# Attention in key steps of 128 with the last 64 keys of two groups in quarters of the array, and a new order of mixing units and norm steps

## The chip, the core and the metric

One core of a Trainium2 chip runs the whole program. TensorE (PE) multiplies: weights are loaded (PEld) and a second operand streams past them into PSUM, which has eight banks. ScalarE (ACT), VectorE (DVE) and GpSimd (POOL) work on what is in SBUF, ACT and DVE on PSUM too; SyncE's queue (SP) issues the transfers. Each engine works through its own instructions in order and waits at semaphores for the others. The metric is the device time of one execution in microseconds (us); lower is better.

## What is computed

```python
scores = q @ k^T / sqrt(64) - log(448)         # 8 batches x 12 heads, 448 x 448, head size 64
attn   = sigmoid(scores)                       # no sum over keys: each key chunk stands alone
x      = attn @ v                              # put together as (8, 448, 768)
u      = x + real(fft over tokens(fft over channels(x)))
un     = (u - mean) / sqrt(var + 1e-6)         # over the 768 channels
out    = u + relu(un @ w_ch1) @ w_ch2          # 768 -> 3072 -> 768
```

## The kernel before

Two heads share the 128 partitions (head j on rows 64j to 64j+63); such a pair is a *group* g, 48 in all, and two groups make a *round* gg of four heads, three rounds to a batch. Queries are stored as 450 columns, since the transform wants tokens n and -n side by side.

**Scores.** `scores` (L124) takes one step t of 112 keys of one group. The operands are split into a high and a low part (`cast` L111 on ACT, `rest` L119 on DVE), and three products are summed: six matmuls at L131, the two heads in the two row halves of the array. Outputs lie in a two-bank PSUM tile `sc`, of which there are two; ACT's sigmoid (L135) turns it into `a`, of which there are six buffers.

**Values.** `values` (L138) follows every fourth step: four chunks of 112 keys times two heads at L148, plain fp32, 64 columns per head, so the two heads stand in the two column halves. Each such fp32 matmul is two instructions in the trace. ACT copies the sum to `xT` (L155).

**Mixing.** When a batch is through, `fold` (L159, POOL and DVE) forms sums and differences `xp`, and `mix_units` (L176) returns a list of small units: 24 `stage_d` (L181, one fp32 matmul each, with an ACT copy `A` after every six), 4 `stage_s` (L194, needing `A`; an ACT copy `Q` or two DVE operations), 8 `add_x` (L209, transposes and a DVE addition `u`, stored to `u_dram`). They share three PSUM tiles `m`. `mix_some` (L428) gives out units worth a budget in estimated us and carries what is not used over to the next call, up to one budget while the list is empty.

**Side work.** `weight` (L248) converts 48 pieces of the feed-forward weights during attention (a load, an ACT step, DVE steps at L268 to L277, a store). `norm` (L345) normalises the first 512 tokens; its step 7 scales rows on DVE and at once asks ACT for a half-precision copy `hl` (L363). `load_qk` (L98) has two buffers and is called three steps ahead of its cast.

**Order.** The loop at L503 writes out all queues: two score steps, then what is due by the table `extra` at these steps (`at`, L469), then in turn mixing units (2.5 us) or a group's values. `pin` (L440) fixes the order on each engine as written. After attention the units of the last batch are given out between the first feed-forward matmuls (L617); the rest of the program (three quarters of the time) is the feed-forward part, which the diff does not touch except for one buffer: the ring `ws` of pool `ws1` (L395), which holds prepared weights `wp`.

Of the kernel before, what the change touches and what calls it, by code (L numbers as in the profile page):

```python
# [18 lines left out]
S = 448  # L19
# [3 lines left out]
D = 64  # L23
DM = 768
DF = 3072
CP = 112
NG = 3
NFC = DF // 128
NCC = DM // 128
LAG = 2  # L30
ABUF = 6
FOLDS = ((10, 11, 13, 14, 18, 19), (18, 19, 20, 21, 22, 23), (24, 24, 25, 25, 26, 26))
LEAD = 4
LNT = 2
UNIT_US = 2.5
ADD_US = 0.5
HELD = 3

# [16 lines left out]
def spectral_attention_ffn(tc, q, k, v, w1, w2, cd, cs, ident_in, out):  # L55
# [8 lines left out]
    with ExitStack() as top:  # L64
# [19 lines left out]
        if True:  # L84
            c1 = mix.enter_context(tc.tile_pool(name="c1", bufs=1, side="right"))
            fx = mix.enter_context(tc.tile_pool(name="fx", bufs=1, side="right"))
            ps_m = mix.enter_context(tc.tile_pool(name="ps_m", bufs=3, space=PSUM, side="right"))
            io = att_ctx.enter_context(tc.tile_pool(name="io", bufs=2))
            wk = att_ctx.enter_context(tc.tile_pool(name="wk", bufs=2))
            ps_sc = att_ctx.enter_context(tc.tile_pool(name="ps_sc", bufs=2, space=PSUM))  # L90
            ps_av = att_ctx.enter_context(tc.tile_pool(name="ps_av", bufs=1, space=PSUM))

            cd_sb = c1.tile([128, 2, 2, 3, 193], F32, name="cd_sb")
            cs_sb = c1.tile([HM, 2, 2, HM], F32, name="cs_sb")
# [2 lines left out]

            def load_qk(g):  # L98
                b, n = divmod(g, 2 * NG)
                qr = io.tile([128, SQ], F32, tag="qr", name="qr")  # L100
                kr = io.tile([128, S], F32, tag="kr", name="kr")
                nc.sync.dma_start(kr, k[b, n])
                nc.sync.dma_start(qr, q[b, n])
                raw[g] = (qr, kr)

            def load_v(gg):
                b, r = divmod(gg, NG)
                vrs[gg] = vr = io.tile([CP, 4, 256], F32, tag="vr", name="vr")
                nc.sync.dma_start(vr, v[b, r])

            def cast(g, n, e=None):  # L111
# [12 lines left out]
            def scores(t):  # L124

                g, c = divmod(t, 4)
                ps = ps_sc.tile([128, 2, 512], F32, tag="sc", name="sc")
                for n, (kn, qn) in enumerate(((0, 0), (0, 1), (1, 0))):
                    for j in range(2):
                        h = slice(j * D, (j + 1) * D)  # L130
                        nc.tensor.matmul(  # L131
                            ps[:CP, j, :SQ], split[g, 1, kn][h, c * CP:(c + 1) * CP], split[g, 0, qn][h],
                            start=(n == 0), stop=(n == 2))
                att[g, c] = a = wk.tile([CP, 2, SQ], F32, tag="a", name="a", bufs=ABUF)
                nc.scalar.activation(  # L135
                    a, ps[:CP, :, :SQ], AF.Sigmoid, bias=-math.log(S), scale=1.0 / math.sqrt(D))

            def values(g):  # L138
                gg, pr = divmod(g, 2)
                b, r = divmod(gg, NG)  # L140
                p = r + 3 * pr
                vr = vrs[gg]
                ps = ps_av.tile([128, 512], F32, tag="av", name="av")
                for c in range(4):
                    a = att.pop((g, c))
                    for j in range(2):
                        h = 2 * pr + j
                        nc.tensor.matmul(  # L148
                            ps[j * D:(j + 1) * D, :SQ], vr[:, c, h * D:(h + 1) * D], a[:, j],
                            start=(c == 0), stop=(c == 3))  # L150
                if r == 0 and pr == 0:
                    xts[b] = (fx.tile([128, 6, 2, HS], F32, tag="xT", name="xT", bufs=2),
                              fx.tile([128, 2, 2, 2, 3, HM], F32, tag="xp", name="xp"))
# [22 lines left out]
            def mix_units(b):  # L176
# [32 lines left out]
                def add_x(kp, r, hf):  # L209
# [14 lines left out]
                    def add():  # L224
# [10 lines left out]
                    dve_next.append(add)  # L235


                res = [(0.33, lambda kp=kp, c=c, par=par, p=p: stage_d(kp, c, par, p))
                       for kp in range(2) for c in (1, 0) for par in range(2) for p in range(3)]
                res += [(0.65, lambda kp=kp, c=c: stage_s(kp, c)) for kp in range(2) for c in (1, 0)]  # L240
                res += [(ADD_US, lambda kp=kp, r=r, hf=hf: add_x(kp, r, hf))
                        for kp in range(2) for r in range(2) for hf in range(2)]
                return res

            wtile = {}
# [99 lines left out]
            def norm(c, i, n, pool):  # L345
                if n == 0:
                    u = pool.tile([128, DM, 2], F32, tag="un", name="un")
                    u = u.rearrange("p n w -> p (n w)").rearrange("p (i n) -> p i n", i=2)
                    r0 = c * TW + i * 128
                    nc.sync.dma_start(u, u_dram[r0:r0 + 256, :].rearrange("(i p) n -> p i n", p=128))  # L350
                    uns[c, i], uns[c, i + 1] = u[:, 0], u[:, 1]
                elif n == 1:
                    stats(c, i % 2, uns[c, i])
                elif n < 7:
                    rsqrt(c, n)
                elif n == 7:
                    u = uns[c, i]
                    scale_rows(c, i % 2, u)
# [4 lines left out]
                    nc.scalar.activation(hl[:, 0], u, AF.Copy)  # L363
                    uns[c, i] = u, hl
                else:
                    u, hl = uns.pop((c, i))
                    nc.vector.tensor_tensor(out=hl[:, 1], in0=u, in1=hl[:, 0], op=ALU.subtract)
                    for n in range(2):
                        nc.sync.dma_start(uts[c][n][:, :, i * 128:(i + 1) * 128], hl[:, n], transpose=True)

            def norm_plan(c, g, pool):

                res = [(0, lambda: norm(c, 2 * g, 0, pool))]
                for j in range(2):
                    i = 2 * g + j
                    res += [(LEAD + j, lambda i=i: norm(c, i, 1, pool)),
                            (7 + LEAD + 2 * j, lambda i=i: norm(c, i, 7, pool)),
                            (8 + LEAD + 2 * j, lambda i=i: norm(c, i, 8, pool))]
                res += [(LEAD + n, lambda n=n: norm(c, 2 * g, n, pool)) for n in range(2, 7)]
                return sorted(res, key=lambda x: x[0])  # L380

# [79 lines left out]
            if G > 2:  # L461
                load_qk(2)
            if GG > 1:
                load_v(1)
            TQ = 4 * G
            TP = TQ - 16
            extra = {}
# [4 lines left out]
            for b in range(B):  # L472
                for r, when in enumerate(FOLDS):
                    for n, t in enumerate(when):
                        e = nc.vector if r == 2 and n % 2 else nc.gpsimd
                        at(24 * b + LAG + t, lambda b=b, r=r, n=n, e=e: fold(b, r, n, e))
                at(24 * b + 27 + LAG, lambda b=b: units.extend(mix_units(b)))
            for gg in range(2, GG):
                at(8 * gg - 8 + LAG, lambda n=gg: load_v(n))
            for g in range(2, G):  # L480
                if g > 2:
# [427 lines left out]
def _layout(q, k, v, w1, w2):  # L909
# [4 lines left out]

    n = np.arange(HS)
    qt, kt = (np.ascontiguousarray(a) for a in (qt[..., np.concatenate([n, -n % S])], kt))
    vt = np.ascontiguousarray(v.reshape(B, 2, NG, 2, 4, CP, D).transpose(0, 2, 5, 4, 1, 3, 6)).reshape(B, NG, CP, 4, 256)
# [52 lines left out]
```

## Time and profile before

| | |
|---|---|
| median of 3 runs | 1672.88 us (1671.16 to 1675.73) |
| the profiled execution | 1672.65 us, span 1670.9 us, mean granted TensorE clock 0.991 |
| the last group of attention's values starts | 442.56 us |
| one ordinary batch in the middle of attention | 53.93 us |
| batches in which tokens are normalised | 61.61 and 61.62 us |

The time is a span plus a little around it. The page gives busy shares of the whole program; what an edit is worth has to be read in the stage it touches, which here is the first 446 us. In the views, "idle before <-releaser" says how long an engine stood still ahead of a group and what ended that.

### The profile page before, as it was taken

The page shows a single profiled execution, that of the slowest core. Times are in us where ns is not written, and L with a number is a line of the kernel's source. Part 1 is how long each engine was busy: PE and PEld are TensorE (multiplying, and loading weights), DVE is VectorE, ACT ScalarE, POOL GpSimd, SP SyncE. Part 2 cuts the span into 40 slices and gives each one's busy share as a digit, 9 for nine tenths or more (in the row PEclk, how much of TensorE's full clock was granted, in tenths as well). Part 3 has the DMA queues.
Part 4 walks back from the last instruction along what each step waited for, and adds up shares of the span by engine and source line. Part 5 has one row for each costly group of instructions (what it writes and reads, how often), then busy time and mean ns, then how long its engine had stood idle before and what let it go on. Part 6 is the DMA issues. An engine that isn't in the chain of part 4 may idle for free.

```text
span 1670.9 us, 28280 instructions
## 1 busy us (share of the span) xinstructions
PE 1612.0 (96%) x11272; PEld 1098.5 (66%) x11272; DVE 1317.4 (79%) x2548; ACT 696.8 (42%) x927; POOL 271.3 (16%) x224
## 2 busy tenths in 40 slices
PE   7999988899989999999999999999999999999998
PEld 3555555455545545777777777777777777777775
DVE  3887798877458875688888888888888888887778
ACT  5766766676544542432233223322332233223221
POOL 1323322322676762000000000000000000000000
PEclk9999999999999999999999999999999999999999
DMA  7777778676287687755665566556655665666561
GB/s 229 278 252 241 245 266 275 201 273 227 89 279 274 245 323 268 300 203 220 242 244 197 225 242 246 197 225 241 244 199 223 241 246 193 229 241 228 208 240 68
DMA packets 85174, 388.69 MB, mean 233 GB/s; under 512 B 14913, under 2 KB 28466, under 8 KB 66482
## 3 DMA queue, kind: packets, MB, share of 16 engines
q1 hardware_dynamic: 85042, 386.89, 63.8%
q8 instruction: 88, 1.44, 0.3%
q14 instruction: 44, 0.36, 0.1%
HBM read 311.36 MB, written 73.92 MB: 231 GB/s over the span
## 4 chain that ended last, share of the span: by engine, by line
PE 77%; DVE 11%; ACT 4%; DMA 3%; issue 3%; POOL 3%; SPq 0%; ACTq 0%; DVEq 0%; POOLq 0%
PE pso L781 28%; PE psf L725 28%; PE av L148 7%; PE sc L131 6%; PE psd L186 3%; POOL wq L409 3%; DVE wp L401 2%; PE po L555 2%; ACT a L135 2%; DMA qr<-q_in 1%; DVE u L225 1%; PE psh L535 1%; PE pst L654 1%; PE pss L197 1%; DVE wt L275 1%
## 5 line engine op out<-in xcount | busy, mean ns | idle before, releaser
L781 PE MATMUL pso<-ws,H 128*128 128x384 f16 x3024 | 507.5, 326 | 1.0 <-DVE H L731 0.9
L725 PE MATMUL psf<-ut,ws 128*128 128x256 f16 x4536 | 506.6, 273 | 1.1 <-DVE ur L576 1.1
L725 PEld LDWEIGHTS <-ws 128*128 128x128 f16 x4536 | 443.9, 98 | 60.2 <-issue 1.4
L781 PEld LDWEIGHTS <-H 128*128 128x128 f16 x3024 | 295.6, 98 | 186.9 <-DVE H L731 1.7
L750 ACT ACTIVATE F<-F 128x1024 f32<-128x1024 f32 x72 | 76.1, 1057 | 400.3 <-DVE F L731 400.3
L796 DVE TENSOR_TENSOR acc<-pso,acc 128x384 f32<-128x384 f32 x399 | 207.1, 549 | 21.6 <-PE pso L781 21.6
L731 DVE TENSOR_TENSOR H<-F,H 128x1024 f16<-128x1024 f32 (+1 forms) x144 | 155.3, 1087 | 54.0 <-ACT H L760 54.0
L135 ACT ACTIVATE a<-sc 112x900 f32<-112x900 f32 x192 | 166.5, 919 | 56.0 <-PE sc L131 56.0
L760 ACT ACTIVATE H<-F 128x1792 f16<-128x1792 f32 x72 | 122.2, 1697 | 106.6 <-DVE F L731 106.6
L731 DVE TENSOR_TENSOR F<-X,psf 128x256 f32<-128x256 f32 x288 | 117.4, 417 | 56.1 <-PE psf L725 52.6
L148 PE MATMUL av<-a,vr 112*64 112x450 f32 x768 | 157.0, 552 | 0.0
L409 POOL TENSOR_TENSOR wq<-wq 128x384 f32<-128x384 f32 x96 | 133.5, 1395 | 59.4 <-DVE wp L401 37.0
L731 DVE TENSOR_TENSOR F<-F 128x256 f32<-128x256 f32 x288 | 109.4, 421 | 20.2 <-ACT F L750 15.6
L399 ACT ACTIVATE wp<-wq,wsc 128x1536 f16<-128x1536 f32 x48 | 74.5, 1571 | 91.9 <-POOL wq L409 90.6
L148 PEld LDWEIGHTS av<-a,vr 112*64 112x64 f32 x768 | 51.2, 137 | 83.9 <-issue 82.5
L731 DVE TENSOR_TENSOR X<-X,psf 128x256 f32<-128x256 f32 x216 | 89.6, 415 | 17.3 <-PE psf L725 13.8
L401 DVE SCALAR_TENSOR_TENSOR wp<-wq,wsc,wp 128x1536 f16<-128x1536 f32 x48 | 92.8, 1959 | 11.9 <-ACT wp L399 11.8
L535 PE MATMUL psh<-ut,wp 128*128 128x512 f16 x432 | 100.1, 381 | 0.3 <-ACT U L655 0.3
L131 PE MATMUL sc<-qh,kh 64*112 64x450 f32 x384 | 82.6, 426 | 15.0 <-ACT a L135 10.6
L555 PE MATMUL po<-wp,hh 128*128 128x256 f16 (+1 forms) x384 | 90.0, 330 | 0.0
L739 ACT ACTIVATE X<-psf 128x256 f32<-128x256 f32 x72 | 27.8, 386 | 147.4 <-PE psf L725 147.4
L131 PEld LDWEIGHTS sc<-qh,kh 64*112 64x112 f32 x384 | 34.4, 176 | 71.2 <-issue 29.9
(84 smaller groups left out, 1679.5 us busy)
## 6 DMA issues: line engine op xcount, KB each, us to landing
ws<-w_dram SPq DMA_DIRECT2D x144, 1344.0 KB, 6.7
wr<-w_in SPq DMA_DIRECT2D x48, 768.0 KB, 6.2
w_dram<-wp SPq DMA_DIRECT2D x24, 1344.0 KB, 10.6
t_dram<-wt SPq DMA_DIRECT2D x48, 384.0 KB, 4.5
wq<-t_dram SPq DMA_DIRECT2D x24, 768.0 KB, 5.9
qr<-q_in SPq DMA_DIRECT2D x48, 225.0 KB, 4.9
kr<-k_in SPq DMA_DIRECT2D x48, 224.0 KB, 5.0
vr<-v_in SPq DMA_DIRECT2D x24, 448.0 KB, 4.1
```

The lines of the kernel that those rows point to most:

```text
L131: nc.tensor.matmul(ps[:CP, j, :SQ], split[g, 1, kn][h, c * CP:(c + 1) * CP], split[g, 0, qn][h], start=(n == 0), stop=(n == 2))
L135: nc.scalar.activation(a, ps[:CP, :, :SQ], AF.Sigmoid, bias=-math.log(S), scale=1.0 / math.sqrt(D))
L148: nc.tensor.matmul(ps[j * D:(j + 1) * D, :SQ], vr[:, c, h * D:(h + 1) * D], a[:, j], start=(c == 0), stop=(c == 3))
L401: nc.vector.scalar_tensor_tensor(out=w[:, 1, part], in0=t, scalar=sc, in1=w[:, 0, part], op0=ALU.mult, op1=ALU.subtract)
L409: nc.gpsimd.tensor_tensor(out=t[:, o], in0=t[:, x], in1=t[:, y], op=op)
L535: nc.tensor.matmul(hs[c, f], l[:, m], r[:, m], start=(m == n == 0), stop=(m == NCC - 1 and n == 2))
L555: nc.tensor.matmul(po[n][:, at:at + hi - lo], l[:, cols], r[:, lo:hi], start=(f == 0 and m == 0 and at == 0), stop=(f == NFC - 1 and m == ...
L725: nc.tensor.matmul(ps[:, :TH], w[:, x, a, m * 128:(m + 1) * 128], ut[y][:, b, m], start=(m == n == 0), stop=(m == n == 2))
L731: nc.vector.tensor_tensor(out=o, in0=x, in1=y, op=op)
L760: nc.scalar.activation(hts[P][:, 0], F[:, 1:8], AF.Copy)
L781: nc.tensor.matmul(ps[:, :384], H[:, x, a, tp * 128:(tp + 1) * 128], w[:, y, b], start=(j == n == 0 and half != 1), stop=(j == 1 and n == ...
L796: later(0, lambda: nc.vector.tensor_tensor(out=to, in0=ps[:, :384], in1=to, op=ALU.add))
```

## The change

Keys are taken as 3 x 128 + 64 instead of 4 x 112. The three steps of 128 work as before (`scores`, `values`). The last 64 keys of the two groups of a round are handled together: `half_scores` puts four plain fp32 matmuls (two groups, two heads; no split) on the four 64 x 64 quarters of the array, followed by one sigmoid; `half_values` does the same for the products with v and opens the sums that `values` then closes. So a round has seven sigmoids instead of eight, and 36 + 4 matmuls for scores instead of 48. The values' sums move to the pool of tiles `m`, which has four tiles now. The loop works in rounds of four parts: part 0 half values and values of the round before and half scores of this one; part 1 two score steps and values; part 2 two score steps and mixing units (4.9 us); part 3 two score steps.

Besides: q and k have four buffers and are loaded ten or more steps ahead of the cast; casts, rests, folds and the start of a batch's mixing units are at other steps; the mixing units come in another order (each `stage_s` some units after the `stage_d` it needs, transposes between); `norm` is stretched, with `hl` two steps after the scaling and the low half and its transposing stores two steps after that; `xp` has no buffer of its own any more but takes one of the three of the ring `ws`.

```diff
-CP = 112
+CP = 128
+CH = 64
-LAG = 2
-ABUF = 6
-FOLDS = ((10, 11, 13, 14, 18, 19), (18, 19, 20, 21, 22, 23), (24, 24, 25, 25, 26, 26))
+ABUF = 7
+FOLDS = ((12, 13, 14, 16, 17, 18), (20, 21, 22, 24, 25, 26), (28, 29, 30, 31, 32, 33))
-UNIT_US = 2.5
+UNIT_US = 4.9
...
-            ps_m = mix.enter_context(tc.tile_pool(name="ps_m", bufs=3, space=PSUM, side="right"))
+            ps_m = mix.enter_context(tc.tile_pool(name="ps_m", bufs=4, space=PSUM, side="right"))
-            ps_av = att_ctx.enter_context(tc.tile_pool(name="ps_av", bufs=1, space=PSUM))
...
-                qr = io.tile([128, SQ], F32, tag="qr", name="qr")
-                kr = io.tile([128, S], F32, tag="kr", name="kr")
+                qr = io.tile([128, SQ], F32, tag="qr", name="qr", bufs=4)
+                kr = io.tile([128, S], F32, tag="kr", name="kr", bufs=4)
...
+            def half_scores(gg):
+                ps = ps_sc.tile([128, 2, 512], F32, tag="sc", name="sc")
+                for x in range(2):
+                    for j in range(2):
+                        w = x ^ j
+                        qr, kr = raw[2 * gg + w]
+                        h = slice(j * D, (j + 1) * D)
+                        nc.tensor.matmul(
+                            ps[w * CH:(w + 1) * CH, j, :SQ], kr[h, 3 * CP:S], qr[h], start=True, stop=True)
+                att[gg] = sigmoid(ps)
+            def half_values(gg):
+                vr, a = vrs[gg], att.pop(gg)
+                avs[gg] = [ps_m.tile([128, 512], F32, tag="m", name="av") for w in range(2)]
+                for x in range(2):
+                    for j in range(2):
+                        w = x ^ j
+                        h = slice(w * CH, (w + 1) * CH)
+                        nc.tensor.matmul(
+                            avs[gg][w][j * D:(j + 1) * D, :SQ], vr[h, 768 + j * D:768 + (j + 1) * D], a[h, j],
+                            start=True, stop=False)
+            def values(gg, w):
...
+                for c in range(3):
+                    a = att.pop((2 * gg + w, c))
                     for j in range(2):
+                        h = c * 256 + (2 * w + j) * D
                         nc.tensor.matmul(
+                            ps[j * D:(j + 1) * D, :SQ], vr[:, h:h + D], a[:, j], start=False, stop=(c == 2))
...
+                    xp = wst[0].tile([128, 2, 8, 384], F16, tag="ws", name="xp", bufs=3)
...
+                last = units_d(1, 0)
+                res = (units_d(0, 1) + units_d(0, 0) + units_d(1, 1) + units_s(0, 1) + last[:3] + units_s(0, 0)
+                       + last[3:] + units_x(0, 0) + units_s(1, 1) + units_x(0, 1) + units_s(1, 0)
+                       + units_x(1, 0) + units_x(1, 1))
...
                             (7 + LEAD + 2 * j, lambda i=i: norm(c, i, 7, pool)),
-                            (8 + LEAD + 2 * j, lambda i=i: norm(c, i, 8, pool))]
+                            (9 + LEAD + 2 * j, lambda i=i: norm(c, i, 8, pool)),
+                            (11 + LEAD + 2 * j, lambda i=i: norm(c, i, 9, pool))]
...
             load_qk(0)
+            load_qk(1)
             load_v(0)
-            load_qk(1)
...
-                at(24 * b + 27 + LAG, lambda b=b: units.extend(mix_units(b)))
+                at(24 * b + 34, lambda b=b: units.extend(mix_units(b)))
...
-                    at(4 * g - 9, lambda g=g: load_qk(g))
-                for n, fn in enumerate((cast, rest)):
-                    at(4 * g - 6 + 2 * n, lambda g=g, fn=fn: (fn(g, 0), fn(g, 1)))
+                    at(8 * gg - 4, lambda n=gg: load_v(n))
+                    at(8 * gg - 14, lambda g=2 * gg: load_qk(g))
+                    at(8 * gg - 13, lambda g=2 * gg + 1: load_qk(g))
+                for w in range(2):
+                    for n, fn in enumerate((cast, rest)):
+                        at(8 * gg - 4 + 2 * n + 2 * w, lambda g=2 * gg + w, fn=fn: (fn(g, 0), fn(g, 1)))
...
-            for t in range(0, TQ + LAG + 4, 2):
+            for t in range(0, TQ + 12, 2):
                 flush(sp_next)
-                for i in range(t, t + 2):
-                    if i < TQ:
-                        scores(i)
+                gg, part = divmod(t // 2, 4)
+                if part == 0:
+                    if 0 < gg <= GG:
+                        half_values(gg - 1)
+                    if gg < GG:
+                        half_scores(gg)
+                elif gg < GG:
+                    scores(gg, 2 * part - 2)
+                    scores(gg, 2 * part - 1)
...
-                if t % 4 == 2:
+                if part < 2:
+                    if 0 < gg <= GG:
+                        values(gg - 1, part)
+                elif part == 2:
                     mix_some(UNIT_US)
-                elif 0 < t <= TQ:
-                    values(t // 4 - 1)
                 pin()
```

More of the change, by code (lines that the diff above doesn't have):

```diff
@@ L107, in load_v @@
                 b, r = divmod(gg, NG)
-                vrs[gg] = vr = io.tile([CP, 4, 256], F32, tag="vr", name="vr")
+                vrs[gg] = vr = io.tile([128, 896], F32, tag="vr", name="vr")
                 nc.sync.dma_start(vr, v[b, r])
@@ L122, in rest, with sigmoid, scores @@
                     out=t, in0=raw[g][n], in1=split[g, n, 0].bitcast(F32), op=ALU.subtract)
-            def scores(t):
-                g, c = divmod(t, 4)
+            def sigmoid(ps):
+                a = wk.tile([CP, 2, SQ], F32, tag="a", name="a", bufs=ABUF)
+                nc.scalar.activation(
+                    a, ps[:, :, :SQ], AF.Sigmoid, bias=-math.log(S), scale=1.0 / math.sqrt(D))
+                return a
+            def scores(gg, n):
+                w, c = divmod(n, 3)
+                g = 2 * gg + w
                 ps = ps_sc.tile([128, 2, 512], F32, tag="sc", name="sc")
@@ L131, in scores @@
                         nc.tensor.matmul(
-                            ps[:CP, j, :SQ], split[g, 1, kn][h, c * CP:(c + 1) * CP], split[g, 0, qn][h],
+                            ps[:, j, :SQ], split[g, 1, kn][h, c * CP:(c + 1) * CP], split[g, 0, qn][h],
                             start=(n == 0), stop=(n == 2))
-                att[g, c] = a = wk.tile([CP, 2, SQ], F32, tag="a", name="a", bufs=ABUF)
-                nc.scalar.activation(
-                    a, ps[:CP, :, :SQ], AF.Sigmoid, bias=-math.log(S), scale=1.0 / math.sqrt(D))
@@ L138, in values @@
-            def values(g):
-                gg, pr = divmod(g, 2)
-                b, r = divmod(gg, NG)
[L141 to L145, printed above, removed]
+                att[g, c] = sigmoid(ps)
+            def half_scores(gg):
[8 more added lines that the diff above has]
+                att[gg] = sigmoid(ps)
@@ new lines, in spectral_attention_ffn @@
+            avs = {}
+            def half_values(gg):
[8 more added lines that the diff above has]
+                            start=True, stop=False)
@@ L146, in values @@
+            def values(gg, w):
+                b, r = divmod(gg, NG)
+                p = r + 3 * w
+                vr, ps = vrs[gg], avs[gg][w]
+                for c in range(3):
+                    a = att.pop((2 * gg + w, c))
                     for j in range(2):
-                        h = 2 * pr + j
+                        h = c * 256 + (2 * w + j) * D
                         nc.tensor.matmul(
-                            ps[j * D:(j + 1) * D, :SQ], vr[:, c, h * D:(h + 1) * D], a[:, j],
-                            start=(c == 0), stop=(c == 3))
@@ L151, in values @@
-                if r == 0 and pr == 0:
+                            ps[j * D:(j + 1) * D, :SQ], vr[:, h:h + D], a[:, j], start=False, stop=(c == 2))
+                if r == 0 and w == 0:
+                    xp = wst[0].tile([128, 2, 8, 384], F16, tag="ws", name="xp", bufs=3)
+                    xp = xp.rearrange("p x s n -> p (x s n)").bitcast(F32)[:, :24 * HM]
                     xts[b] = (fx.tile([128, 6, 2, HS], F32, tag="xT", name="xT", bufs=2),
-                              fx.tile([128, 2, 2, 2, 3, HM], F32, tag="xp", name="xp"))
+                              xp.rearrange("p (f c r i s) -> p f c r i s", f=2, c=2, r=2, i=3))
@@ L235, in add_x, with units_d, units_s, units_x @@
                     dve_next.append(add)
[L238 to L242, printed above, removed]
+                def units_d(kp, c):
+                    return [(0.33, lambda par=par, p=p: stage_d(kp, c, par, p)) for par in range(2) for p in range(3)]
+                def units_s(kp, c):
+                    return [(0.65, lambda: stage_s(kp, c))]
+                def units_x(kp, r):
+                    return [(ADD_US, lambda hf=hf: add_x(kp, r, hf)) for hf in range(2)]
+                last = units_d(1, 0)
+                res = (units_d(0, 1) + units_d(0, 0) + units_d(1, 1) + units_s(0, 1) + last[:3] + units_s(0, 0)
+                       + last[3:] + units_x(0, 0) + units_s(1, 1) + units_x(0, 1) + units_s(1, 0)
+                       + units_x(1, 0) + units_x(1, 1))
                 return res
@@ L356, in norm @@
                 elif n == 7:
+                    scale_rows(c, i % 2, uns[c, i])
+                elif n == 8:
                     u = uns[c, i]
-                    scale_rows(c, i % 2, u)
                     if i == 0:
@@ L460, in spectral_attention_ffn @@
                 rest(g, 1)
[L461 to L464, printed above, removed]
+            load_qk(2)
+            load_qk(3)
+            load_v(1)
             TQ = 4 * G
@@ L475, in spectral_attention_ffn @@
                         e = nc.vector if r == 2 and n % 2 else nc.gpsimd
-                        at(24 * b + LAG + t, lambda b=b, r=r, n=n, e=e: fold(b, r, n, e))
-                at(24 * b + 27 + LAG, lambda b=b: units.extend(mix_units(b)))
[L478 to L481, printed above, removed]
-                    at(4 * g - 9, lambda g=g: load_qk(g))
-                for n, fn in enumerate((cast, rest)):
-                    at(4 * g - 6 + 2 * n, lambda g=g, fn=fn: (fn(g, 0), fn(g, 1)))
+                        at(24 * b + t, lambda b=b, r=r, n=n, e=e: fold(b, r, n, e))
+                at(24 * b + 34, lambda b=b: units.extend(mix_units(b)))
+            for gg in range(1, GG):
+                if gg > 1:
+                    at(8 * gg - 4, lambda n=gg: load_v(n))
[4 more added lines that the diff above has]
+                        at(8 * gg - 4 + 2 * n + 2 * w, lambda g=2 * gg + w, fn=fn: (fn(g, 0), fn(g, 1)))
             at(6, lambda: (nc.sync.dma_start(cd_sb, cd), nc.sync.dma_start(cs_sb, cs)))
@@ L916, in _layout @@
     qt, kt = (np.ascontiguousarray(a) for a in (qt[..., np.concatenate([n, -n % S])], kt))
-    vt = np.ascontiguousarray(v.reshape(B, 2, NG, 2, 4, CP, D).transpose(0, 2, 5, 4, 1, 3, 6)).reshape(B, NG, CP, 4, 256)
+    vt = v.reshape(B, 2, NG, 2, S, D)
+    full = vt[..., :3 * CP, :].reshape(B, 2, NG, 2, 3, CP, D).transpose(0, 2, 5, 4, 1, 3, 6).reshape(B, NG, CP, 768)
+    half = vt[..., 3 * CP:, :].transpose(0, 2, 1, 4, 3, 5).reshape(B, NG, CP, 128)
+    vt = np.ascontiguousarray(np.concatenate([full, half], axis=-1))
     w1t = np.ascontiguousarray(w1.reshape(NCC, 128, NFC, 128).transpose(1, 2, 0, 3)).reshape(128, -1).view(np.int64)
```

## The prediction

> **What bounds the kernel now.** I read the busy shares first, then a table of windows cut at the same place of six successive batches, then PE's timeline inside one batch.
>
> ```profile
> PE 1612.0 (96%) x11272; PEld 1098.5 (66%) x11272; DVE 1317.4 (79%) x2548; ACT 696.8 (42%) x927; POOL 271.3 (16%) x224
> ...
> core 0: us, PE busy (x) PEld busy (x) DVE busy (x) ACT busy (x) POOL busy (x), PEclk, DMA share, GB/s
> 69.35:124.89 55.54, 52.67 (x322) 30.22 (x324) 43.48 (x63) 38.02 (x56) 16.68 (x15) 0.97 0.73 250
> 124.89:178.82 53.93, 51.04 (x322) 29.84 (x324) 43.32 (x63) 38.00 (x56) 16.71 (x15) 1.00 0.73 254
> 232.75:294.36 61.61, 52.89 (x321) 30.68 (x322) 53.96 (x92) 39.15 (x58) 16.73 (x15) 0.94 0.77 248
> 294.36:355.98 61.62, 52.94 (x324) 30.78 (x324) 54.07 (x91) 39.35 (x58) 16.69 (x15) 0.94 0.77 240
> 355.98:409.90 53.92, 51.04 (x323) 29.86 (x324) 41.89 (x60) 37.21 (x55) 17.05 (x16) 1.00 0.67 228
> ```
>
> In an ordinary batch PE works 51.04 of 53.93 us: PE bounds it, and work taken from PE counts. In the two batches with norms (232.75 to 355.98) PE stands about 8.7 us each, and DVE, at 54, could not follow a PE much faster.
>
> ```profile
> 113.39 0.60 PE L148 MATMUL av<-a,vr 112*64 112x450 f32 x2
> 113.82 0.55 PE L148 MATMUL av<-a,vr 112*64 112x450 f32 x2
> 113.82 0.93 PE L148 MATMUL av<-a,vr 112*64 112x450 f32 x4
> ...
> 113.09 0.37 PE L131 MATMUL sc<-qh,kl 64*112 64x450 f32 x2
> 113.39 3.24 PE L148 MATMUL av<-a,vr 112*64 112x450 f32 x16
> 116.56 0.46 PE L131 MATMUL sc<-qh,kh 64*112 64x450 f32 x2
> 116.86 0.37 PE L131 MATMUL sc<-ql,kh 64*112 64x450 f32 x2
> 117.07 0.37 PE L131 MATMUL sc<-qh,kl 64*112 64x450 f32 x2
> 117.27 0.37 PE L131 MATMUL sc<-qh,kh 64*112 64x450 f32 x2
> 117.48 0.36 PE L131 MATMUL sc<-ql,kh 64*112 64x450 f32 x2
> 117.68 0.37 PE L131 MATMUL sc<-qh,kl 64*112 64x450 f32 x2
> 117.98 5.50 PE L186 MATMUL psd<-cd_sb,xp 128*113 128x193 f32 x32
> ...
> 155.80 1.25 PE L218 MATMUL psx<-ident,xT 128*112 128x128 f32 x9
> ```
>
> Rows give start, length, engine, line. Score matmuls start two at a time, the two heads side by side, every 0.205 us: a step's three pairs cost 0.62. Values too start in pairs, one instruction per column half; a pair more lengthens a group from 0.55 to 0.93, so a slot of two costs 0.38, and a group's 16 instructions are 8 slots, 3.04 of the 3.17 us between 113.39 and 116.56. The first score pair after other work takes 0.30, and so does the last ahead of it (117.68 to 117.98): an excursion from scores and back costs 0.10 + 0.13 + 0.10, about 0.32. Such a batch has six for values and five for mixing (the first and last are quoted).
>
> **PE's work in an ordinary batch.** Score steps fall from 24 to 18: 6 x 0.62 = 3.7 less. Values fall from 48 slots to 36: 4.6 less. Six blocks of quarter matmuls come in (half scores, half values, three of each), each four fp32 matmuls of 450 columns, two instructions apiece. No row shows four tiles at work at once; rows show two row halves (L131) and two column halves (L148). With all four at once a block is 2 slots, 0.76; two at a time, 4 slots, 1.52; one after another, 8 slots, 3.04. I take 0.76: each row half writes a bank of its own and the four tiles share nothing that the two-tile rows do not share. That is 4.6 more. Excursions fall from eleven to eight, with three inner switches (0.15): 0.5 less. Sum: -3.7 - 4.6 + 4.6 - 0.5 = -4.2.
>
> The Trainium skill, "TensorEngine Tiling (Array Packing)", Tiling Modes, says that 64x64 gives four independent tiles; by that a block is 0.76 too. The same section says that changing the mode drains the engine; the 0.30 of the first pair agrees.
>
> ```profile
> L186 PEld LDWEIGHTS psd<-cd_sb,xp 128*113 128x113 f32 x304 | 49.1, 177 | 6.8 <-issue 5.4
> L148 PEld LDWEIGHTS av<-a,vr 112*64 112x64 f32 x560 | 37.1, 136 | 60.2 <-issue 60.1
> L131 PEld LDWEIGHTS sc<-qh,kh 64*112 64x112 f32 x268 | 23.7, 174 | 40.4 <-issue 24.1 <-ACT a L135 9.5 <-ACT kh L114 1.7
> L654 PEld LDWEIGHTS pst<-ident,U 128*128 128x128 f32 x24 | 2.8, 141 | 5.8 <-DVE hl L543 5.1
> ```
>
> **Wider weights.** Score loads grow from 112 to 128 columns. From 64 to 112 columns a load grows from 136 to 174 ns, 0.79 per column: 16 more are 13 ns, and on 432 pairs (144 steps) that is +5.5 us if loads set the pitch. But the one 128-column fp32 load, L654, takes 141; then a pair could fall to 0.19, half a slot, -6.5 us. I take 0: L186's load (177) is longer than the 163 ns between its matmuls (32 in 5.50 us less the switch and the last one's tail) and does not hold them.
>
> The Trainium skill, "TensorE: Matmul & The Clock Gate", LDWEIGHTS, gives columns / 1.2 ns: +13 ns here, by which the sum would be 5.8 us worse, an estimate; L654's 141 ns speaks against it.
>
> **Stalls of an ordinary batch.**
>
> ```profile
> 140.57 1.55 PE L197 MATMUL pss<-A,cs_sb 113*112 113x385 f32 x4 [0.80 <-ACT A L190]
> 158.66 0.59 PE L218 MATMUL psx<-ident,xT 128*112 128x128 f32 x3 [1.61 <-DVE u L225]
> 165.72 0.46 PE L131 MATMUL sc<-qh,kh 64*112 64x450 f32 x2 [0.47 <-ACT a L135]
> ...
> 315.88 1.62 PE L197 MATMUL pss<-A,cs_sb 113*112 113x385 f32 x2 [6.60 <-ACT A L190]
> ...
> 310.87 0.84 ACT L363 ACTIVATE hl<-un 128x768 f16<-128x768 f32 x1 [5.95 <-DVE un L341]
> ```
>
> The 0.80 goes: `stage_s` now has five or more units between it and the last `stage_d` it needs. The 1.61 stays, since eight transposing units still share four tiles with DVE's additions behind. The 0.47 grows. `mix_some` carries one unused budget, so 9.8 us of units come in the first call, the rest in the second and none in the third (the 32 instructions at 117.98, 16 units for a budget of 2.5, show the carry today). So every third round has no mixing between its steps, and with two tiles `sc` PE waits for sigmoids: I take 1.0 us. Together +0.3, so about -4.0 per ordinary batch; bounds -5 (no new stall) and -2.5. The folds, moved by up to nine steps, cost nothing: POOL works 16.7 us of a batch, three buffers for `xp` end its waits for PE, and after the last fold's step PE has half a round's values and four score steps, some 7 us, ahead of the first unit. If DVE, which does half of the last folds, lags by more, that unit waits for the rest.
>
> **Norm batches.** PE's 6.60 us wait is for `A`, which stands on ACT behind `hl`, which waited 5.95 us for DVE's scaling. `hl` now comes two steps later (4.5 us at 53.93 per 24), so most of it goes; late next is DVE itself, 54.0 us. I take 55.5 for 61.6: -6.1, twice -12.2. Bounds: 50 (DVE's weight steps slip into the next batch) and 57.4 (the wait stays, PE's 4.2 goes). Behind `hl` on SP stand its transposing stores and then loads of q, k and weights; with four buffers q and k have ten steps to land.
>
> **The start.**
>
> ```profile
> 11.52 3.17 PE av L148 x16
> 19.51 11.42 DMA qr<-q_in
> 57.76 2.41 PE av L148 x11
> ...
> 44.31:57.76 13.45, 12.52 (x83) 5.85 (x84) 13.31 (x16) 10.40 (x15) 7.89 (x7) 1.00 0.76 277
> ...
> L135 ACT ACTIVATE a<-sc 112x900 f32<-112x900 f32 x25 | 21.7, 918 | 9.6 <-PE sc L131 9.6
> ```
>
> Until the first units a round takes 13.45 us (the window is two groups). PE's part falls by a third of 4.2 to 11.1, ACT's by one sigmoid (0.87 of the 10.40) to 9.5; with waits for sigmoids I take 12.3, four rounds: -4.6. Between 11.52 and 57.76 lie six groups, 40.4 us at that pace; they took 46.2, and the chain names a load of q that took 11.42 us. Issued ten steps ahead, I count 4 of the 5.9 as gone, and +1.6 because the first half scores need both groups' loads: -2.4. Start: -7, bounds -10 and -2 (DMA share is 0.76 at 277 GB/s there; if it is full, the pace stays).
>
> **The end of attention.**
>
> ```profile
> 442.56 3.24 PE L148 MATMUL av<-a,vr 112*64 112x450 f32 x16
> 445.73 4.06 PE L535 MATMUL psh<-ut,wp 128*128 128x512 f16 x18
> 449.62 3.48 PE L186 MATMUL psd<-cd_sb,xp 128*113 128x193 f32 x20
> 452.94 0.81 PE L535 MATMUL psh<-ut,wp 128*128 128x512 f16 x3
> ```
>
> The last two rounds save 1.35 each: -2.7. Then units and feed-forward matmuls alternate as before; the first call gives 17 units (4.9 carried and 0.65, against the 10 at 449.62), so the last `stage_d` is out before ACT asks for the third `wp`, which takes the buffer of this batch's `xp`. I count 0, with +8 if ACT does stand there with `A` and `Q` behind it. The feed-forward part follows as it is, earlier.
>
> **Sum**, against the profiled execution's 1672.65: start -7, four ordinary batches -16, two with norms -12.2, end -2.7: -37.9, that is 1634.8; the median of the runs is 0.2 above that execution: 1635.
>
> **Rivals.** *Quarters two at a time*: a block is 1.52, 48 blocks cost 36 more, of which about 10 lie under DVE in the norm batches and under ACT at the start: 1661. For it: only two at once is ever seen. Against: rows and columns split independently in the rows above. *One after another*: 3.04 a block, 109 more, 14 of it hidden: 1730, slower than before. It decides from about 1.8 us a block (37.9 over the 36 blocks outside the norm batches is 1.05, above 0.76); the place is the 4 x 2 instructions, if a tile's second instruction holds back the others. Against it: at 113.39 both halves start at once though each has two instructions. *DVE or ACT becomes the bound in every batch*: DVE works 43.3 of 53.93 now; if 8 of its 10.6 idle us are waits that stay, ordinary batches end at 51.3 and norm batches at 58, and the third `wp` costs 6: 5.6 + 5 + 6 more, 1652. *The order does not do what it says* (`hl` still blocks): 57.4, only 4 more.
>
> **Chances.** Four at once 0.71 with 1615 to 1650 as its own range (norm batches at 50, shorter loads and a better start, -21; their opposites, +15); DVE or ACT 0.11; two at a time 0.12; one after another 0.06. The range 1616 to 1662 leaves out the last and the edges. Faster by over 0.3% (below 1667.9; about what a measurement here can tell from no change) 0.87, within 0.05, slower 0.08.
>
> **What would show it.** Right: quarter matmuls starting four at a time, blocks of 0.8 us; batches of 50 us with PE at 47; norm batches near 55 with DVE above 95% and no wait of 6 us on `A`. Wrong: quarters starting in twos; score pairs off 0.205; PE waiting for `a` or `u` by several us per batch; ACT standing before `wp` at the end of attention.

## The result and the profile after

The changed kernel takes 1636.12 us (median of 4 runs, 1632.57 to 1637.70), the one before 1672.70 beside it: a ratio of 0.9776, 95% interval 0.9754 to 0.9798. The profiled execution took 1635.05 with a span of 1633.3, 37.6 us under the span of before. First the busy shares of the page, then windows cut at the half values of every third round: two ordinary batches, the two with norms, one more ordinary. The columns are as in the table of before.

```profile
PE 1580.8 (97%) x11176; PEld 1083.7 (66%) x11176; DVE 1306.9 (80%) x2548; ACT 675.6 (41%) x903; POOL 273.9 (17%) x224
```

```profile
108.98:159.30 50.32, 47.04 (x310) 28.04 (x309) 41.24 (x63) 35.25 (x54) 16.81 (x16) 1.00 0.80 275
159.30:209.85 50.55, 47.09 (x310) 28.05 (x308) 41.23 (x63) 35.48 (x54) 16.80 (x16) 1.00 0.80 275
209.85:264.98 55.13, 48.82 (x311) 28.87 (x309) 51.67 (x92) 36.10 (x56) 17.33 (x16) 0.97 0.82 274
264.98:322.71 57.73, 50.21 (x311) 30.23 (x309) 51.65 (x93) 36.96 (x57) 16.56 (x16) 0.95 0.81 280
322.71:372.30 49.59, 47.20 (x311) 28.24 (x309) 39.65 (x62) 34.52 (x53) 16.67 (x15) 0.99 0.77 264
```

An ordinary batch went from 53.9 to 50.3, PE's work in it from 51.0 to 47.0. The timeline of PE at the seam of two rounds shows the new blocks:

```profile
159.30 0.98 PE L163 MATMUL av<-a,vr 64*64 64x450 f32 x8
161.05 1.08 PE L150 MATMUL sc<-qr,kr 64*64 64x450 f32 x8 [0.76 <-ACT a L125]
162.06 2.49 PE L175 MATMUL av<-a,vr 128*64 128x450 f32 x12
164.48 0.47 PE L137 MATMUL sc<-qh,kh 64*128 64x450 f32 x2
164.79 0.36 PE L137 MATMUL sc<-ql,kh 64*128 64x450 f32 x2
164.99 0.38 PE L137 MATMUL sc<-qh,kl 64*128 64x450 f32 x2
...
208.22 0.47 PE L137 MATMUL sc<-qh,kh 64*128 64x450 f32 x2 [1.61 <-ACT a L125]
```

L163 is the half values, L150 the half scores, L175 the values, L137 the scores. Eight instructions of four quarters lie within 0.98 us, of which the last one's tail is some 0.17 as everywhere: two slots, so all four quarters run at once. (A single row of the same trace shows four starts 6 to 7 ns apart, at 108.985, 108.991, 108.998 and 109.005, and the next four 0.43 later.) Score pairs still follow each other every 0.20 to 0.21 us. The largest idle places left in an ordinary batch are before the half scores (0.76) and in the round without mixing units (1.61).

### The profile page after: what moved, and what is told of

It reads as the page before. It is cut to its first block, busy times and chain, and to the rows that moved or that the text cites. A ratio compares the mean times of both kernels' runs of the same rounds, so it can differ in the third digit from the quotient of the medians.

```text
span 1633.3 us, 28067 instructions
## 1 busy us (share of the span) xinstructions
PE 1580.8 (97%) x11176; PEld 1083.7 (66%) x11176; DVE 1306.9 (80%) x2548; ACT 675.6 (41%) x903; POOL 273.9 (17%) x224
## 4 chain that ended last, share of the span: by engine, by line
PE 64%; DVE 5%; POOL 1%; ACT 1%; issue 1%; ACTq 0%; DVEq 0%; POOLq 0%
PE pso L826 29%; PE psf L770 29%; PE po L600 3%; PE psh L580 2%; DVE wp L439 2%; POOL wq L447 1%; PE pst L699 1%; DVE F L776 1%; ACT wp L437 0%; DVE H L776 0%; DVE U L377 0%; ACT H L805 0%; DVE ur L621 0%; DVE ur L854 0%; DVE ut L716 0%
## 5 line engine op out<-in xcount | busy, mean ns | idle before, releaser
L125 ACT ACTIVATE a<-sc 128x900 f32<-128x900 f32 x168 | 147.3, 923 | 46.4 <-PE sc L137 39.5
L175 PE MATMUL av<-a,vr 128*64 128x450 f32 x576 | 121.1, 557 | 0.0
L175 PEld LDWEIGHTS av<-a,vr 128*64 128x64 f32 x576 | 37.6, 138 | 71.4 <-issue 71.4
L195 POOL TENSOR_TENSOR eo<-xT 128x450 f32<-128x450 f32 x40 | 44.4, 1127 | 218.8 <-ACT xT L183 211.4
L137 PE MATMUL sc<-qh,kh 64*128 64x450 f32 x288 | 63.0, 433 | 13.7 <-ACT a L125 13.6
```

The lines of the kernel that those rows point to most:

```text
L125: nc.scalar.activation(a, ps[:, :, :SQ], AF.Sigmoid, bias=-math.log(S), scale=1.0 / math.sqrt(D))
L175: nc.tensor.matmul(ps[j * D:(j + 1) * D, :SQ], vr[:, h:h + D], a[:, j], start=False, stop=(c == 2))
```

## The experiments

All ratios are to the kernel before, run beside each on the same chip; the changed kernel's is 0.9776, and kernels are compared by their ratios. A batch is measured from one place of the loop to the same place three rounds later.

**keys_of_112: the new order without the packing.**

```diff
-CP = 128
...
+CP = 112
...
-ABUF = 7
+ABUF = 10
...
-                        half_values(gg - 1)
...
-                        half_scores(gg)
...
+                    scores(gg, 2 * part)
+                    scores(gg, 2 * part + 1)
```

> The changed kernel's order of work (loop in rounds, mixing units, norm steps, loads ahead, four shared sum tiles, xp in the ring of prepared weights), but keys again as 4 x 112 with eight sigmoids a round and no quarter matmuls (q and k have three buffers instead of four, for room). Theory A, the array packing carries most of the gain: ordinary batches are back near 54 us, the norm batches keep about 4 us each of their gain and the start 2 to 3, so about 1662 us (1655 to 1668). Theory B, the order carries it: 1645 or less.

Measured: 1670.9 us, ratio 0.9986 (0.9975 to 0.9997). Theory A's direction, but above its range (1655 to 1668): without the quarters the whole reordering is worth about 2 us. Its ordinary batches got longer than before, not equal. Windows of its three rounds, then the end of the third in finer windows:

```profile
124.97:149.50 24.53, 24.12 (x140) 15.71 (x138) 12.97 (x21) 13.18 (x21) 7.22 (x7) 0.92 0.50 177
149.50:167.32 17.82, 16.36 (x104) 8.92 (x102) 12.67 (x23) 11.88 (x19) 5.92 (x6) 1.00 0.74 250
167.32:182.87 15.55, 13.41 (x82) 6.63 (x80) 13.11 (x19) 12.84 (x18) 1.97 (x2) 0.91 0.97 333
```

```profile
174.00:180.00 6.00, 4.21 (x30) 2.00 (x26) 3.80 (x7) 5.31 (x8) 1.97 (x2) 1.00 1.00 341
180.00:184.00 4.00, 3.65 (x16) 2.21 (x18) 3.93 (x7) 3.77 (x6) 0.30 (x1) 0.50 0.95 353
184.00:188.00 4.00, 4.00 (x16) 1.09 (x12) 3.93 (x6) 0.92 (x1) 1.01 (x1) 0.65 0.95 334
```

In the empty round ACT works 12.84 of 15.55 us, PE waits for sigmoids, and then the granted clock falls to 0.50 and 0.65 for some 6 us. PE's busy time in a batch, 53.89 us, is larger than before (51.04) with the same matmuls. Whether the empty round is the cause is what keys_of_112_spread, below, is for.

**half_scores_twice: 24 blocks more.**

```diff
-                for x in range(2):
+                for x in (0, 1, 0, 1):
```

> The changed kernel with every block of four quarter matmuls for the half scores written twice over (24 more blocks of 0.76 us; the second overwrites the first with the same numbers). Theory A, TensorE sets the pace in the rounds that hold mixing units and not in the third rounds, where it waits for sigmoids: +8 to +16 us over the changed kernel's 1636, so 1644 to 1652. Theory B, VectorE or ScalarE has become the bound everywhere: at most +4.

Measured: 1641.85 us, ratio 0.9812 (0.9794 to 0.9829), 0.0036 or 6 us over the changed kernel: between the two theories. By rounds, A's rule holds. Three rounds of a batch took 22.63, 16.60 and 12.29 us against 21.90, 15.86 and 12.56: +0.73, +0.74 and nothing in the round where PE waits anyway. The two norm batches took nothing either (110.6 us together against 112.9), which is why the sum fell short. So two rounds in three, outside the norms, are bound by PE.

**norm_as_before.**

```diff
-                            (9 + LEAD + 2 * j, lambda i=i: norm(c, i, 8, pool)),
-                            (11 + LEAD + 2 * j, lambda i=i: norm(c, i, 9, pool))]
+                            (7 + LEAD + 2 * j, lambda i=i: norm(c, i, 8, pool)),
+                            (8 + LEAD + 2 * j, lambda i=i: norm(c, i, 9, pool))]
```

> The changed kernel with the norm steps at the old distances (hl asked for at the step of the scaling, low half and stores one step later). Theory A, ScalarE standing behind hl was most of the norm batches' loss: these two batches grow by 2 to 6 us each, 1640 to 1648 in all, with a TensorE wait for A or a of several us in each. Theory B, VectorE's 52 us of work sets these batches: within 2 us of 1636.

Measured: 1645.20 us, ratio 0.9830 (0.9814 to 0.9847), 9 us more; the norm batches are back at 61.86 and 60.91. ACT's and PE's rows:

```profile
231.52 0.84 ACT L400 ACTIVATE hl<-un 128x768 f16<-128x768 f32 x1 [8.92 <-DVE un L377]
292.53 0.84 ACT L400 ACTIVATE hl<-un 128x768 f16<-128x768 f32 x1 [7.86 <-DVE un L377]
...
293.82 1.63 PE L225 MATMUL pss<-A,cs_sb 113*113 113x385 f32 x2 [5.16 <-ACT A L218]
```

Theory A: ACT's wait at `hl`, 6 us before the change, is 8 to 9 in the faster kernel when `hl` comes at the old distance.

**units_spread: units in every round.**

```diff
-                paced[0] = paced[0] + us if units else min(paced[0] + us, us)
+                paced[0] = paced[0] + us if units else 0.0
...
-                for step, e in enumerate((0, 8, 9)):
+                for step, e in enumerate((0, 8 + 4 * p, 9 + 4 * p)):
```

> The changed kernel with no budget carried into a batch's first call, so that mixing units come as 4.9 us in each of three rounds instead of 9.8, 4.7 and 0 (the second early wp is prepared four steps later, so that it does not stand ahead of units it needs). Theory A, the 2.3 us per batch that TensorE waits for sigmoids in the third round are the price of the empty round: seven batches, -8 to -16, 1620 to 1628. Theory B, the waits only move and the third excursion per batch is added: 1634 to 1640.

Measured: 1637.25 us, ratio 0.9781 (0.9764 to 0.9798): no change, as theory B has it, but not by its mechanism. The last half values start at 396.80 instead of 408.09: attention did gain what A said. It was given back after it, where ACT stood still:

```profile
422.02 0.52 ACT L218 ACTIVATE A<-psd 113x386 f32<-113x386 f32 x1
431.52 3.04 ACT L437 ACTIVATE wp<-wq,wsc 128x1536 f16<-128x1536 f32 x2 [8.98 <-DMA w_dram<-wp]
434.47 0.47 ACT L229 ACTIVATE Q<-pss 113x385 f32<-113x385 f32 x1
```

The view puts the wait down to a store of an earlier `wp`, and the times agree: that store was issued at 422.05 (0.62 us) and such a store takes 8.8 us to land. The prediction's bound of +8 named another candidate, the third `wp` in the buffer of the last `xp`; but the last `stage_d`, which reads `xp`, had ended by 426.8, 4.7 us before the wait did. With nothing carried over, two units go out per call after attention, so the last `stage_d` stands behind this `wp` in the written order. My reading, which no view shows directly, is that the ring could not yet give out `xp`'s buffer and gave out the one that the store was still reading.

**spread_then_carry: one line more.**

```diff
+            paced[0] = UNIT_US
             while units or act_next or dve_next or sp_next:
```

> units_spread again, but with one budget of 4.9 us put back before the first call after attention, so that 17 units go out at once there as in the changed kernel. Theory A, units_spread gained its 7 to 11 us inside attention and lost them after it, where ScalarE stood 9 us ahead of the third wp until the last stage_d had left xp: the fourth feed-forward block starts near 438 instead of 445, and the time is 1626 to 1631. Theory B, what was lost after attention is due to something else (weights prepared late for a start 7 us earlier): 1634 to 1638 as before.

Measured: 1625.37 us, ratio 0.9716 (0.9700 to 0.9731). Theory A, 0.6 us below its range: the last half values start at 394.38, the fourth feed-forward block (each has 18 `psh` matmuls) at 433.93. From the first block to the fourth it takes 29.87 us, units_spread 39.32. The third `wp` no longer waits, although the store, issued at 419.58 here, was still under way if it took 8.8 us again:

```profile
422.43 3.04 ACT L437 ACTIVATE wp<-wq,wsc 128x1536 f16<-128x1536 f32 x2
```

So with the last `stage_d` written ahead of it, the third `wp` does not wait for that store. The loss was at the ring which `wp` and `xp` share, by way of the store, and not, as the expectation had it, a wait until `xp` was read.

**keys_of_112_spread: the edits of the last two runs without the packing.**

> keys_of_112 (the new order without quarter matmuls) with its mixing units spread as in spread_then_carry. In keys_of_112 every third round, empty of units, ends in TensorE waits of about 2 us for sigmoids and then some 5 us at a granted clock of 0.5 to 0.65. Theory A, the empty round and the clock behind it make the new order alone worthless: with units in every round ordinary batches fall from 57.9 to 53 to 55 with the clock at 1.00, and the time from 1671 to 1645 to 1655. Theory B, without the quarters ScalarE's eight sigmoids a round set the pace whatever the units do: at most 5 us less than keys_of_112.

Measured: 1658.74 us, ratio 0.9917 (0.9900 to 0.9933). Two of its ordinary batches, and the same two of spread_then_carry:

```profile
120.96:174.25 53.29, 51.03 (x323) 30.05 (x321) 42.84 (x63) 37.67 (x56) 17.42 (x15) 1.00 0.77 261
174.25:227.58 53.33, 51.06 (x322) 30.07 (x320) 42.86 (x63) 37.77 (x56) 17.42 (x15) 1.00 0.80 263
```

```profile
106.84:156.35 49.51, 47.07 (x310) 28.08 (x308) 42.48 (x64) 35.24 (x53) 18.18 (x15) 1.00 0.80 279
156.35:205.46 49.11, 46.66 (x310) 28.19 (x309) 42.41 (x64) 35.25 (x53) 18.24 (x15) 1.00 0.80 284
```

The clock is at 1.00, the batch went from 57.9 to 53.3, PE's busy time back to 51.03. Theory A's mechanism; its time came out 4 us above its range. With units in every round the packing is worth 3.8 to 4.2 us per ordinary batch (4.0 to 4.4 of PE's busy time), the sum worked out in the prediction. With the empty round it was worth 7.6, since without the packing ACT's eighth sigmoid and the clock behind the waits came on top. Over the whole kernel the packing is worth some 34 us in either order (0.9986 to 0.9776, 0.9917 to 0.9716). With units in every round about 8 us of that lie in the start (66.12 against 56.70, less 1.6 for two more score steps), where the runs of 112 also have only three buffers for q and k; how much of it is the buffers no run separates.

**loads_late, units_old_order, rows_share_bank: one part each.**

```diff
-                    at(8 * gg - 14, lambda g=2 * gg: load_qk(g))
-                    at(8 * gg - 13, lambda g=2 * gg + 1: load_qk(g))
+                    at(8 * gg - 7, lambda g=2 * gg: load_qk(g))
+                    at(8 * gg - 5, lambda g=2 * gg + 1: load_qk(g))
```

> The changed kernel with q and k loaded three steps ahead of their cast, as before (four buffers kept). Theory A, loads ahead of time end waits that stood in the chain: 3 to 10 us more than 1636, with ScalarE waits for q and TensorE waits behind them. Theory B, the loads had been hidden but for the start: within 2 us.

Measured: 1631.97 us, ratio 0.9757 (0.9741 to 0.9773). Theory B by its time, and if anything it is faster: 3.2 us by the ratios, within their intervals. The traces show the same 3.2 us at one place, the start: step 32 comes at 54.16 instead of 57.40, on which more below.

```diff
-                last = units_d(1, 0)
-                res = (units_d(0, 1) + units_d(0, 0) + units_d(1, 1) + units_s(0, 1) + last[:3] + units_s(0, 0)
-                       + last[3:] + units_x(0, 0) + units_s(1, 1) + units_x(0, 1) + units_s(1, 0)
-                       + units_x(1, 0) + units_x(1, 1))
+                res = (units_d(0, 1) + units_d(0, 0) + units_d(1, 1) + units_d(1, 0)
+                       + units_s(0, 1) + units_s(0, 0) + units_s(1, 1) + units_s(1, 0)
+                       + units_x(0, 0) + units_x(0, 1) + units_x(1, 0) + units_x(1, 1))
```

> The changed kernel with the mixing units in their old order (24 stage_d, four stage_s, eight transposing units). Theory A, given out in one burst a stage_s finds its A ready in either order, and the new order pays only after attention, where ScalarE is busy with wp: 0 inside attention, 3 to 6 us after it, 1639 to 1642. Theory B, the order ends the 0.8 us wait of every batch: 6 us inside attention as well, 1643 to 1648.

Measured: 1642.62 us, ratio 0.9820 (0.9794 to 0.9846). Neither as stated: in the profiled execution (1639.71) two ordinary batches together took 100.6 us against 100.9, so nothing there (A), but after attention the loss to the fourth block was only 1 us; the norm batches together took 3.6 more, with PE waits for `ql` from DVE. Why the order matters just there stays open, and so does what made two of the four runs longer still (1645.54 and 1646.95).

```diff
-                            ps[w * CH:(w + 1) * CH, j, :SQ], kr[h, 3 * CP:S], qr[h], start=True, stop=True)
+                            ps[w * CH:(w + 1) * CH, x, :SQ], kr[h, 3 * CP:S], qr[h], start=True, stop=True)
...
-                            avs[gg][w][j * D:(j + 1) * D, :SQ], vr[h, 768 + j * D:768 + (j + 1) * D], a[h, j],
+                            avs[gg][w][j * D:(j + 1) * D, :SQ], vr[h, 768 + j * D:768 + (j + 1) * D], a[h, x],
```

> The changed kernel with the half scores' two banks exchanged for one group, so that in each pair of diagonal quarters the two row halves write the same PSUM bank at the same time (half values read accordingly). Theory A, separate banks for the row halves are what lets four quarters run at once: blocks of half scores grow from 0.76 to about 1.5 us, +5 to +9 us going by half_scores_twice. Theory B, banks do not matter for writes to different partitions: blocks of 0.76, within 2 us of 1636.

Measured: 1635.88 us, ratio 0.9783 (0.9763 to 0.9802). Theory B; the block is as long as with separate banks:

```profile
159.51 1.08 PE L150 MATMUL sc<-qr,kr 64*64 64x450 f32 x8 [0.76 <-ACT a L125]
160.52 2.49 PE L175 MATMUL av<-a,vr 128*64 128x450 f32 x12
```

**Going on: spread_folds_pool and spread_folds_pool_wr.** What was left in spread_then_carry was mostly PE's idle time before a batch's first units (waits for `xp` from DVE, 12.8 us in six places).

```diff
-FOLDS = ((12, 13, 14, 16, 17, 18), (20, 21, 22, 24, 25, 26), (28, 29, 30, 31, 32, 33))
+FOLDS = ((12, 13, 14, 16, 17, 18), (20, 21, 22, 24, 25, 26), (28, 28, 28, 30, 30, 30))
...
-                        e = nc.vector if r == 2 and n % 2 else nc.gpsimd
+                        e = nc.gpsimd
```

> spread_then_carry with all six last folds of a batch on GpSimd (three of them were VectorE's), asked for at steps 28 and 30. Theory A, the waits left in front of a batch's first units (12.8 us in six batches for xp from VectorE) are VectorE's queue: they go, and VectorE loses 3 us a batch: 5 to 12 us less than spread_then_carry's 1625. Theory B, GpSimd's chain of six, about 7 us, is no faster: within 3 us.

Measured: 1618.28 us, ratio 0.9674 (0.9659 to 0.9688). Theory A, 7 us; the waits for `xp` are gone from the table of waits. Then the weights' loads:

```diff
-                for step, d in enumerate((-8, -4, -2, 0, 2)):
+                for step, d in enumerate((-10, -4, -2, 0, 2)):
```

> spread_folds_pool with each piece of the weights loaded two steps earlier. Theory A, ScalarE's waits for these loads (16 us in the changed kernel) stand ahead of sigmoids and reach TensorE: 2 to 6 us less than spread_folds_pool. Theory B, they are slack, or the earlier loads only crowd the others: within 2 us, or more.

Measured: 1614.57 us, ratio 0.9653 (0.9638 to 0.9667). Theory A, 4 us: ACT's waits for these loads up to 400 us fell from 14.4 to 4.7 us, and an ordinary batch is at 47.6:

```profile
106.46:154.09 47.63, 46.63 (x311) 28.21 (x309) 39.38 (x61) 35.26 (x53) 20.20 (x18) 1.00 0.83 291
201.71:253.64 51.93, 49.60 (x311) 28.57 (x309) 50.56 (x90) 37.09 (x55) 20.82 (x17) 0.97 0.79 260
```

PE works 46.63 of 47.63 there: what is left in ordinary batches is PE's work itself.

## Why the prediction was right, and where its terms were off

It said 1635 (1616 to 1662); 1636.1 was measured. By the same cuts in the two profiled executions, with the cut at step 32 brought to the same work as told below:

| term | predicted | measured | from |
|---|---|---|---|
| start, to step 32 | -7 | about -1.9 | 59.3 (an estimate, see below) to 57.40 |
| four ordinary batches | -16 | -15.3 | -4.0, -3.6, -3.4, -4.3 |
| two norm batches | -12.2 | -10.4 | 61.69 to 55.13, 61.56 to 57.73 |
| end of attention | -2.7 | about -4.5 | what is left of the spans' -37.6 |
| after attention | 0 | -5.6 | see below |

**PE's work** (-4.2 a batch) came out: 51.04 to 47.04, and four quarters at once, of which the prediction was least sure, are seen directly. The price of an excursion (0.30 or 0.31 for the first pair) and the budget carried into an empty third round came out too.

**The stalls** came out in their sum: 3.3 us of idle time in an ordinary batch, as predicted (2.9 and 0.3 more). The parts did not. The waits for sigmoids are 2.3 us (1.5 in the empty round and 0.76 before the half scores) where 0.47 and 1.0 more were taken, and the transposing units wait 1.0 instead of 1.61. The 0.80 for `A` is gone, but units_old_order shows no such wait in its ordinary batches either, so the new order of the units is not needed for that.

**Wider weights** were rightly set to 0, for the reason given. The group of the changed kernel's loads:

```profile
L137 PEld LDWEIGHTS sc<-qh,kh 64*128 64x128 f32 x288 | 27.7, 188 | 59.7 <-ACT a L125 26.0 <-issue 22.4 <-ACT wt L299 8.5
```

A load grew from 174 to 188 ns, as the row-to-row slope had it (13 ns), while the pitch of score pairs stayed at 0.20 to 0.21 us. The faster 128-column load of L654 did not carry over to these.

**The norm batches** came out in the first (55.13 for 55.5) and were mis-sized in the second (57.73, above even the bound of 57.4). `hl` was the cause of the old loss (norm_as_before), but after it came more than DVE's load, and DVE is busy for 94 and 89% of these batches, not above 95:

```profile
248.14 2.64 PE L246 MATMUL psx<-ident,xT 128*112 128x128 f32 x12 [3.20 <-DVE u L253]
278.48 7.83 PE L214 MATMUL psd<-cd_sb,xp 128*113 128x193 f32 x36 [2.38 <-DVE xp L201]
320.22 0.68 PE L137 MATMUL sc<-qh,kh 64*128 64x450 f32 x2 [3.36 <-ACT a L125]
```

```profile
318.03 0.89 ACT L299 ACTIVATE wt<-wr 128x768 f32<-128x768 f32 x1 [3.46 <-DMA wr<-w_in]
```

The first two are DVE in arrears, as foreseen; the third is a load of weights, four steps ahead of its use, which four steps no longer covered. The 36 instructions at 278.48 take 7.83 us where an ordinary batch (169.78) takes 6.16: after a wait the granted clock is down (0.67 from 278 to 282).

**The start** is where the prediction failed most, and a cut hides it. At step 32 the kernel before stands at 69.28 and the changed one at 57.40, but the kernel before has done more work by then: 5.4 us of mixing units, the values of a seventh group, and two more score steps. Values now trail by a round and not by a group, and stand ahead of the round's scores. The rows are these values, the first pair of the two steps after them, the units, and the first pair of the two steps after those:

```profile
57.69 3.24 PE L148 MATMUL av<-a,vr 112*64 112x450 f32 x16
60.86 0.46 PE L131 MATMUL sc<-qh,kh 64*112 64x450 f32 x2
62.45 5.50 PE L186 MATMUL psd<-cd_sb,xp 128*113 128x193 f32 x32
67.88 0.46 PE L131 MATMUL sc<-qh,kh 64*112 64x450 f32 x2
```

With the same work done, it would stand near 59.3: 57.69, where the seventh group's values start after 30 steps, and 1.59 (60.86 to 62.45) for the next two steps. That is an estimate; by it the start gave about 2 us, not 7. The pace was right: rounds of 11.81 and 12.63 us (from 14.42 and from 44.77) for the 12.3 taken. What failed is the step that 4 of the 5.9 us behind the load of q would go. The round between those two, from 26.23, took 18.54, six more than its neighbours:

```profile
29.31 0.89 ACT L299 ACTIVATE wt<-wr 128x768 f32<-128x768 f32 x1 [3.02 <-DMA wr<-w_in]
31.07 1.87 PE L150 MATMUL sc<-qr,kr 64*64 64x450 f32 x8 [3.85 <-ACT a L125]
```

ACT stands for a load of weights where it stood for q, PE stands for the sigmoid behind it, and the granted clock of that round is 0.82. In loads_late the same round takes 14.45 with a clock of 1.00, and ACT waits 1.8 us for q and 0.3 for weights up to 60 us. Step 32 comes at 54.16 there, and at 56.1 to 58.2 in the changed kernel and the other variants whose start is written the same. So the early loads of q and k did not shorten the start but cost it 2 to 4 us; that they hold up the weights' load beside them is likely and not shown.

**The end of attention** has the same work in it the other way round. After the last scores stand 5.6 us of half values and values (408.09 to 413.69) instead of 3.2, but that is work that the start's cut leaves out and not a loss. What is left of the difference of the spans is about 4.5 us for 2.7, since at equal work the last window holds the scores of two rounds but the values of three, and the prediction counted two of each.

**After attention** the prediction took 0 and the stage gave 5.6 (from the first feed-forward block to the first `psf` matmul: 445.73 to 664.37 before, 413.69 to 626.75 after). To the fourth block:

```profile
445.73:482.53 36.80, 31.41 (x154) 19.78 (x153) 20.25 (x22) 15.40 (x17) 29.05 (x21) 0.95 0.54 180
```

```profile
413.69:445.02 31.33, 29.41 (x154) 19.27 (x153) 20.70 (x22) 13.96 (x16) 24.13 (x19) 1.00 0.50 160
```

The same 154 matmuls; PE's idle time falls from 5.4 to 1.9 and the clock stays up, since 17 units ahead of the rest leave no `stage_s` waiting for its `A` behind ACT's `wp` (PE waited 4.4 us for `A` there before, and does not now). The guess that ACT does not stand before the third `wp` was right here and would not have been with another carry (units_spread).

Start and norm batches gave 5 and 2 us less than predicted, the end and the time after attention 2 and 6 us more. That the total is off by only 1 us is luck; the total is no proof of each term.

**The rivals**: two at a time and one after another are refuted by the rows of L163; that DVE or ACT bounds every batch is refuted by half_scores_twice, for two rounds of three. That `hl` still blocks is refuted too: the second norm batch took as long as that rival had it, but no PE wait for `A` stands in it.

## What to carry to other kernels

Four fp32 matmuls that each fill a quarter of the array took the slots of one here: count slots, not matmuls. Where the order of work is written out by hand, an edit that empties one round of filler makes another engine the bound there, and a wait can cost twice, once as idle time and once as a slow clock after it. When a gain inside a stage does not reach the end, look at the first wait after the stage: here a ring of buffers with two uses held 9 us that one line gave back. And when two kernels are compared stage by stage, see that both have done the same work at the cut.

## What the runs showed of the hardware that was not expected

Waits of 0.46 and 1.68 us for sigmoids within 4 us were followed by a granted clock of 0.50 to 0.65 for about 6 us (keys_of_112, 180 to 188). The Trainium skill, "TensorE: Matmul & The Clock Gate", Part 1, has the clock fall after an idle window of about 3.4 us; half speed agrees, but the longest idle stretch here was 1.7 us, so no unbroken wait of that length came before it.

Two row halves that write one PSUM bank at the same time did not slow each other (rows_share_bank, 1.08 us for the block either way). The Trainium skill, "TensorEngine Tiling (Array Packing)", Restrictions and Gotchas, says that different row tiles cannot access the same bank simultaneously; this run, with different partitions of the bank, shows nothing of that in the time.
